# Batches 0 and 1 of a packed attention with routed experts: keys turned in thirds, values in one transfer a group

## The chip, the cores and the metric

The kernel runs on one core of one Trainium2 chip. The metric is the device time of one execution in microseconds, median of three runs. Of the engines, the TensorE (PE) multiplies and transposes, VectorE (DVE), ScalarE (ACT) and GpSimd (POOL) do the element work, and SyncE (SP) mostly issues DMA transfers.

## What is computed

Eight batches of attention with eight heads, 576 tokens of 64 columns, and 32 packed rows a head; then a mixture of experts over the 4608 rows, whose router picks one of 8 experts:

```python
def _attn_ref(q, k, v, p):                       # q, k, v: 8 x 8 x 576 x 64, p: 8 x 8 x 32 x 64
    p_packed = sm_attn(p, k, v)                  # packed rows attend to the tokens
    return sm_attn(q, p_packed, p_packed)        # tokens attend to the packed rows

def _moe_ref(x, expert_emb, tau, w1, w2):        # x: 4608 x 512, w1: 8 x 512 x 1024, w2: 8 x 1024 x 512
    xn, en = x / (norm(x) + 1e-6), expert_emb / (norm(expert_emb) + 1e-6)
    logits = xn @ en.T / tau
    expert_idx = argmax(logits)
    for e in range(8):
        h = maximum(x[mask(e)] @ w1[e], 0.0)
        out[mask(e)] = gate_w[mask(e), None] * (h @ w2[e])
```

## The kernel before

The kernel takes the batches one after the other. For each it guesses the one expert of the batch, loads that expert's weights and computes attention and the expert's two layers; a branch at the end repairs rows for which the guess was wrong. The expert's layers fill the TensorE (`ffn`: lines 1065, 1100, 1118), and the attention of the next batch is put between their matmuls, step by step, by tables (`PLAN` for batch 0) and counters. The order of every engine's instructions is the order in which the code records them.

Batches 0 and 1 start differently from the rest, in `begin`. Four heads form a group, and a batch has two groups. `load_whole` brings one group's keys (or queries) in one transfer of 576 KB into a tile `nat` of 128 partitions: a partition holds one head's 18 successive tokens, 64 columns each. The TensorE turns blocks of 128 columns (two tokens) of it into a PSUM bank (`turn`, line 1265), and ScalarE or VectorE copies the bank into `kT` (in the tile `spare`). `parity_scores` (line 1297) then multiplies the turned packed rows (`wp`, made by `scaled` and `packed_turn`) with the keys of one head, odd and even tokens apart. For batch 0 the keys are turned in nine blocks a group, four at a time (`turn_keys` with `blocks`, which gives the blocks in the order 0, 3, 6, 1, 4, 7, 2, 5, 8), so that a head's columns in `kT` come in 32s and nine such runs are read in a row. Then come the maxima (line 452), the exponentials (458), turns of these (473), and the products with the values (486), from which the packed rows, the guess of the expert (638, 653) and the loads of its weights (952, 960) follow. Before all this the TensorE runs two matmuls on a tile of ones (`WARM`, line 1253).

`load_v` brings a group's values for the products at line 486: a tile of 96 partitions of which each third of 32 comes in its own transfer of 192 KB, three a group. For batch 0 one of the three is issued on ScalarE's queue, all others on SP's. The values of batch 1 and its queries (`load_nat`, four transfers of 140 KB a tile to 32 partitions each) are issued on SP after the weights of batch 0's expert. VectorE turns those queries (`flip`, line 298, tile `kt`), and the TensorE scores them at line 277.

After its first stretch `begin` goes on in steps that `PLAN` places: it turns batch 1's keys with five banks and copies, all copies on ScalarE, and scores them, while the first layer's rows of batch 0 are made (`rows_w1`, line 1033).

PSUM banks: `pf` has three, `pu` one of one bank, `pt` two of two banks each. A bank that comes around again waits for its copy. Transfers issued on SP and ACT carry one of eight completion semaphores in turn (DMAHW0 to DMAHW7 below), and a transfer that takes one again waits on its engine for the landing of the one that had it before.

## Time and profile before

| | us |
|---|---|
| median of 3 runs | 412.96 (412.46 to 413.61) |
| the profiled execution | 413.71 |
| its span | 412.0 |
| TensorE busy | 403.6 (98%) |
| VectorE busy | 310.5 (75%) |
| ScalarE busy | 203.6 (49%) |
| GpSimd busy | 161.7 (39%) |

The span runs from the first to the last instruction of the profiled execution; times in the rows below count from its start. The busy time of the TensorE is that of its matmuls, whose ends are modelled, so waits of a few tenths of a microsecond can lie inside it. The chain that ended last is 89% TensorE work; 7% of it are DMA transfers, all of these in the first 50 us.

### The profile page before, as it was taken

Reading aid. Unit: us, or ns where it says so; the run is one execution under the profiler, and the core shown is the slowest. Engines: PE = TensorE matmul, PEld = TensorE weight load, DVE = VectorE, ACT = ScalarE, POOL = GpSimd, SP = SyncE. Lnnn points to the kernel's source line nnn. Section 1 sums busy time; section 2 is a strip of 40 time slices with the busy share of each in tenths; the row PEclk is TensorE's granted clock in tenths of the full one; section 3 lists DMA queues with packets and bytes.
Section 4 is the critical chain, followed back from the end, with each engine's and each line's share of the span. In section 5 each row is a group of like instructions: output and inputs, shape, how many; then the busy total and the mean of one; then the engine's idle time right before and its main releaser. Section 6 shows DMA issues by size and latency. Waiting matters only on the chain.

```text
span 412.0 us, 11101 instructions
## 1 busy us (share of the span) xinstructions
PE 403.6 (98%) x4012; PEld 322.5 (78%) x4013; DVE 310.5 (75%) x984; ACT 203.6 (49%) x507; POOL 161.7 (39%) x202
## 2 busy tenths in 40 slices
PE   8999999999999999999999999999999999999995
PEld 4758588797878978698786978789687987879785
DVE  3577888589996889779896899868897798836700
ACT  4677454763257622765138622667237641475201
POOL 2355802337503474047703375035730477030500
PEclk9999999999999999999999999999999999999999
DMA  8999888876699679985799768995798722910022
GB/s 226 334 331 214 218 279 297 218 203 183 227 333 241 170 192 336 286 205 139 222 396 234 181 167 273 324 234 136 210 335 281 203 60 81 391 35 19 9 61 56
DMA packets 42607, 87.93 MB, mean 213 GB/s; under 512 B 11690, under 2 KB 20906, under 8 KB 42546
## 3 DMA queue, kind: packets, MB, share of 16 engines
q1 hardware_dynamic: 35280, 61.44, 53.8%
q0 software_dynamic: 6720, 25.17, 16.7%
q10 hardware_dynamic: 546, 0.54, 0.6%
q8 instruction: 34, 0.56, 0.6%
q14 instruction: 27, 0.22, 0.2%
HBM read 77.68 MB, written 9.44 MB: 211 GB/s over the span
## 4 chain that ended last, share of the span: by engine, by line
PE 89%; DMA 7%; SPq 1%; issue 0%; DVE 0%; ACT 0%; DVEq 0%; ACTq 0%
PE pf L1118 43%; PE pf L1065 22%; PE pf L1100 6%; PE pt L995 3%; PE pt L797 3%; DMA w2r<-in_moe_w 2%; DMA vn<-in_v 2%; PE pt L403 2%; DMA nat<-in_q 2%; PE pt L277 2%; PE pt L338 2%; PE pu L797 2%; PE pf L1253 1%; PE pf L1265 1%; SPq L952 0%
## 5 line engine op out<-in xcount | busy, mean ns | idle before, releaser
L1118 PE MATMUL pf<-w2s,hT 128*128 128x512 f32 (+1 forms) x792 | 181.8, 387 | 0.0
L1118 PEld LDWEIGHTS pf<-w2s,hT 128*128 128x128 f32 x792 | 143.6, 188 | 39.2 <-issue 10.7
L971 POOL TENSOR_TENSOR w2s<-w2r,w2s 128x512 fp32r<-128x512 f32 x64 | 80.8, 1286 | 73.0 <-ACT w2s L970 68.2
L1065 PE MATMUL pf<-AT,G 128*128 128x288 f32 x720 | 102.1, 298 | 0.4 <-DVE hT L1070 0.2
L1065 PEld LDWEIGHTS pf<-AT,G 128*128 128x128 f32 x720 | 97.2, 188 | 4.3 <-issue 1.5
L1070 DVE SCALAR_TENSOR_TENSOR hT<-pf,hT 128x224 fp32r<-128x224 f32 (+1 forms) x128 | 52.2, 413 | 29.1 <-ACT hT L1069 28.7
L1069 ACT ACTIVATE hT<-pf 128x224 fp32r<-128x224 f32 (+1 forms) x128 | 49.2, 385 | 42.9 <-PE pf L1065 40.2
L298 DVE STREAM_TRANSPOSE kt<-nat 128x576 f32<-128x576 f32 x52 | 38.0, 757 | 2.3 <-DMA nat<-in_q 2.0
L1475 ACT ACTIVATE o<-pf,gate 128x512 f32<-128x512 f32 (+1 forms) x41 | 25.9, 633 | 24.6 <-PE pf L1118 17.1
L970 ACT CAST w2s<-w2r 128x512 fp32r<-128x512 f32 x64 | 37.7, 623 | 0.0
L891 POOL MEMSET oh<- 64x8 f32 x8 | 0.8, 98 | 86.1 <-DVE oh L887 86.1
L716 ACT ACTIVATE st<-st 128x576 f32<-128x576 f32 (+1 forms) x17 | 11.1, 658 | 43.7 <-DVE st L713 42.6
L1100 PE MATMUL pf<-w2r,h 128*64 128x256 f32 x256 | 31.5, 385 | 0.0
L1008 DVE TENSOR_TENSOR G<-pt,G 128x1024 fp32r<-128x1024 f32 x14 | 16.5, 1220 | 15.7 <-ACT G L1007 15.7
L933 ACT ACTIVATE lg<-lg 128x40 f32<-128x40 f32 x8 | 1.9, 237 | 48.4 <-DVE lg L929 48.4
L390 POOL TENSOR_TENSOR qs<-p 128x320 f32<-128x320 f32 x12 | 10.5, 876 | 36.9 <-ACT p L371 36.9
L1100 PEld LDWEIGHTS pf<-w2r,h 128*64 128x64 f32 x256 | 16.9, 137 | 8.5 <-PE pu L510 1.0
L810 ACT ACTIVATE scr<-pt 128x512 f32<-128x512 f32 (+1 forms) x32 | 15.7, 490 | 13.8 <-DVE part L851 10.6
L737 ACT CAST AT<-at 128x576 fp32r<-128x576 f32 x15 | 10.1, 674 | 17.9 <-DVE at L731 17.8
L371 ACT ACTIVATE p<-pt,qnm 128x160 f32<-128x160 f32 x48 | 17.7, 397 | 0.0
L960 POOL DMA_DIRECT2D w2r<-in_moe_w x24 | 17.0, 721 | 0.0
L702 DVE STREAM_TRANSPOSE st<-pt 128x288 f32<-128x288 f32 x32 | 13.3, 451 | 0.9 <-PE pt L1297 0.9
(235 smaller groups left out, 520.1 us busy)
## 6 DMA issues: line engine op xcount, KB each, us to landing
nat<-in_q SPq DMA_DIRECT2D x112, 140.0 KB, 3.4
nat<-in_k SPq DMA_DIRECT2D x96, 140.0 KB, 3.2
w1t<-in_moe_w POOLq DMA_DIRECT2D x12, 1024.0 KB, 7.1
w2r<-in_moe_w POOLq DMA_DIRECT2D x24, 512.0 KB, 9.6
out<-o SPq DMA_DIRECT2D x124, 64.0 KB, 2.3
w2r<-in_moe_w SPq DMA_DIRECT2D x8, 512.0 KB, 10.0
vn<-in_v SPq DMA_DIRECT2D x24, 160.0 KB, 3.8
vn<-in_v SPq DMA_DIRECT2D x48, 80.0 KB, 3.7
```

The source lines that it names most:

```text
L298: nc.vector.transpose(kt.rearrange("p (c i) -> p c i", i=32), t)
L371: nc.scalar.activation(x.p1[g][:, n * QW : n * QW + QW], area(x, g)[:, n // 2, n % 2], AF.Exp, bias=x.nm[:, at : at + 1],)
L797: nc.tensor.matmul(to, x.at[at, g, tokens], x.ppx[at, g], start=True, stop=True, tile_position=(64 * half, column),)
L960: queue.dma_start(t, w2e[:, 2 * i : 2 * i + 2, :])
L970: nc.scalar.copy(t[:, 0], raw)
L971: nc.gpsimd.tensor_tensor(out=t[:, 1], in0=raw, in1=t[:, 0].bitcast(F32), op=ALU.subtract)
L1065: nc.tensor.matmul(pf[:, :HS], w, r, start=(n == 0), stop=(n == len(ops) - 1))
L1069: nc.scalar.activation(hT[:, 0, f, cs], pf[:, :n], AF.Relu)
L1070: nc.vector.scalar_tensor_tensor(out=hT[:, 1, f, cs], in0=pf[:, :n], scalar=0.0, in1=hT[:, 0, f, cs].bitcast(F32), op0=ALU.max, op1=ALU.su ...
L1100: nc.tensor.matmul(pf[64 * hf : 64 * hf + 64, :256], h4[:, f], x.w2r[f // 2][:, f % 2, hf * 256 : hf * 256 + 256], start=(f == 0), stop=(f ...
L1118: nc.tensor.matmul(pf[:, :w], hT[:, a, f, c * P : (c + 1) * P], x.w2s[f][:, m, at : at + w], start=(f == 0 and i == 0), stop=(f == NF - 1 ...
L1475: nc.scalar.activation(o[:, :w], pf[:, :w], AF.Copy, scale=x.gate[:, c : c + 1])
```

## The change

Four things are changed, all in batches 0 and 1.

- `load_whole` can load a tile in two parts; batch 0's keys of group 0 come as columns 0 to 383 and the rest, those of group 1 as columns 0 to 767 and the rest.
- Keys are turned in thirds: three successive blocks of 128 go to one bank and one copy of 384 columns. Batch 0 then uses `one_bank` and `bank` in turn, batch 1 six banks instead of five. A head's columns are now read with a stride: `(a c r i)` as `c i a`, the third `a` innermost, 384 columns (1536 bytes) from one element to the next.
- `load_v` lays six successive tokens on a partition, and a group's 96 partitions come in one transfer of 576 KB on SP's queue.
- Order and size: the packed rows are turned first, the scores of group 0 stand ahead of the last third of group 1, and the second matmul of `WARM` has 128 columns instead of 512.

```diff
-    def load_whole(src, g):
+    def load_whole(src, g, split=0):
         t = sb.tile([P, NCB * D], F32, name="nat", tag="nat", bufs=4)
         s = src[g * HB : (g + 1) * HB].rearrange("h (i c) d -> h i (c d)", c=NCB)
-        nc.sync.dma_start(t, s.rearrange("h i w -> (h i) w"))
+        s = s.rearrange("h i w -> (h i) w")
+        for cs in (slice(0, split), slice(split, NCB * D)) if split else (slice(0, NCB * D),):
+            nc.sync.dma_start(t[:, cs], s[:, cs])
...
-    def load_v(b, g, odd=nc.sync):
+    def load_v(b, g):
         t = sb.tile([P, KC * HB * D], F32, name="vn", tag="vn", bufs=2)
         t = t.rearrange("p (h w) -> p h w", h=HB)
-        s = v[b, g * HB : (g + 1) * HB].rearrange("h (i c) d -> i h (c d)", c=NCB)
-        for a in (0, 2, 1):
-            (odd if a == 2 else nc.sync).dma_start(
-                t[32 * a : 32 * a + 32], s[:, :, a * KC * D : (a + 1) * KC * D]
-            )
+        s = v[b, g * HB : (g + 1) * HB].rearrange("h (p c) d -> p h (c d)", c=KC)
+        nc.sync.dma_start(t[:KR], s)
...
-        kn = [load_whole(k[0], g) for g in range(NG)]
+        kn = [load_whole(k[0], g, (g + 1) * 3 * P) for g in range(NG)]
...
-        vn = [load_v(0, g, nc.scalar) for g in range(NG)]
+        vn = [load_v(0, g) for g in range(NG)]
...
-        def parity_scores(to, w, t, g, at):
-            t = t[:, g].rearrange("p (c r i) -> p c r i", r=HB, i=32)
+        def parity_scores(to, w, t, at, g):
...
-                        t[hs, :, head(g, c)],
+                        t[hs, head(g, c)],
...
+        def turn_keys(nat, g, a, pu, copy):
+            turn(nat, pu, range(3 * a, 3 * a + 3))
+            copy(kT[:, g, 3 * a * P : 3 * a * P + 3 * P], pu[:, : 3 * P])
+
+        def key_scores(x, w, g):
+            t = kT[:, g].rearrange("p (a c r i) -> p r c i a", a=3, c=3, r=HB)
+            parity_scores(x.s1[g], w, t, lambda c: head(g, c), g)
+
+        wx = packed_turn(scaled(pn, nc.vector), one_bank())
...
-        for n in range(2 * NG):
-            if n:
+        for n in range(3 * NG):
+            turn_keys(kn1[n // 3], n // 3, n % 3, bank(), nc.scalar.copy)
+            if n not in (0, 3):
                 yield
-            pu = bank()
-            turn(kn1[n // 2], pu, blocks(n % 2 * 4, n % 2 * 4 + 4))
-            nc.scalar.copy(kT[:, n // 2, n % 2 * 512 : n % 2 * 512 + 512], pu)
...
-    WARM = (4, 4)
+    WARM = (4, 1)
```

The line numbers of the changed kernel are one to nine lower or higher than before from there on (1265 is 1264, 1297 is 1292, 1440 is 1307). Three places show what moves. The first is the TensorE's queue at the start, from the turn of the packed rows to the scores of batch 0's second group; `nat_130` and `nat_132` (`nat_133` after) are the keys of groups 0 and 1, `pt` the score banks. Before:

```order
L1283 MATMUL pu_193<-ident_75,wp_158 128x128 [waits DVE_49]
L1283 MATMUL pu_193<-ident_75,wp_158 128x128
L1265 MATMUL pf_197<-ident_75,nat_132 128x128 [waits DMAHW4_49,PE_49]
L1265 MATMUL pf_197<-ident_75,nat_132 128x128 x3
L1265 MATMUL pf_203<-ident_75,nat_132 128x128 [waits Activation_49]
L1265 MATMUL pf_203<-ident_75,nat_132 128x128
L1265 MATMUL pu_207<-ident_75,nat_132 128x128 [waits Activation_49]
L1265 MATMUL pu_207<-ident_75,nat_132 128x128 x2
L1297 MATMUL pt_177<-spare_157,wp_158 32x288 [waits DVE_49]
L1297 MATMUL pt_177<-spare_157,wp_158 32x288 x7
L1297 MATMUL pt_178<-spare_157,wp_158 32x288 [waits DVE_49,Activation_49]
```

And after:

```order
L1264 MATMUL pf_191<-ident_75,nat_130 128x128 [waits PE_49]
L1264 MATMUL pf_191<-ident_75,nat_130 128x128 x2
L1264 MATMUL pu_196<-ident_75,nat_133 128x128 [waits DMAHW5_49,Activation_49]
L1264 MATMUL pu_196<-ident_75,nat_133 128x128 x2
L1264 MATMUL pf_201<-ident_75,nat_133 128x128 [waits DVE_49]
L1264 MATMUL pf_201<-ident_75,nat_133 128x128 x2
L1292 MATMUL pt_179<-spare_155,wp_156 32x288 [waits DVE_49,Activation_49]
L1292 MATMUL pt_179<-spare_155,wp_156 32x288 x7
L1264 MATMUL pu_214<-ident_75,nat_133 128x128 [waits DMAHW6_49,Activation_49]
L1264 MATMUL pu_214<-ident_75,nat_133 128x128 x2
L1292 MATMUL pt_180<-spare_155,wp_156 32x288 [waits DVE_49,Activation_49]
```

The scores of group 0 have moved ahead of the last three turns of group 1, which wait for a part of their own (DMAHW6); the packed rows' turn has moved to the very start.

The second is SP's queue behind the last weight transfer of batch 0's expert: values (`vn`) and first queries (`nat`) of batch 1. Before:

```order
L960 DMA w2r_428<-in_moe_w2 128x2x512 [waits DMAHW7_49]
L232 DMA vn_430<-in_v 32x4x384 [waits DMAHW0_49,PE_49]
L232 DMA vn_430<-in_v 32x4x384 [waits DMAHW1_49]
L232 DMA vn_430<-in_v 32x4x384 [waits DMAHW2_49]
L232 DMA vn_434<-in_v 32x4x384 [waits DMAHW3_49,PE_49]
L232 DMA vn_434<-in_v 32x4x384 [waits DMAHW4_49]
L232 DMA vn_434<-in_v 32x4x384 [waits DMAHW5_49]
L201 DMA nat_438<-in_q 32x1120 [waits DMAHW6_49,PE_49]
L201 DMA nat_438<-in_q 32x1120 [waits DMAHW7_49]
```

And after:

```order
L959 DMA w2r_427<-in_moe_w2 128x2x512 [waits DMAHW5_49]
L233 DMA vn_429<-in_v 96x4x384 [waits DMAHW6_49,PE_49]
L233 DMA vn_431<-in_v 96x4x384 [waits DMAHW7_49,PE_49]
L201 DMA nat_433<-in_q 32x1120 [waits DMAHW0_49,PE_49]
L201 DMA nat_433<-in_q 32x1120 [waits DMAHW1_49]
```

Six transfers of values are two, so the first query transfer comes four transfers sooner; its semaphore was DMAHW6, that of the third second-layer weight transfer, and is now DMAHW0, that of the third first-layer one.

The third is ScalarE's queue where it copies batch 1's turned keys into `spare`, between the turned packed rows (`wp`) and the first layer's rows (`g`). Before:

```order
L1285 COPY wp<-pf 128x2x128 [waits PE_49]
L1434 COPY spare<-pf 128x2x128 [waits PE_49,Activation_49]
L1440 COPY spare<-pf 128x512 [waits PE_49]
L716 ACTIVATE st<-st 128x288 [waits Pool_49] x2
L1440 COPY spare<-pf 128x512 [waits PE_49] x3
L1045 COPY g_550<-pf 128x512 [waits PE_49] x2
```

And after:

```order
L1281 COPY wp<-pf 128x2x128 [waits PE_49]
L1307 COPY spare<-pf 128x384 [waits PE_49]
L1307 COPY spare<-pf 128x384 [waits PE_49,Activation_49]
L715 ACTIVATE st<-st 128x288 [waits Pool_49] x2
L1307 COPY spare<-pf 128x384 [waits PE_49]
L1307 COPY spare<-pf 128x384 [waits PE_49,Activation_49]
L1307 COPY spare<-pf 128x384 [waits PE_49]
L1307 COPY spare<-pf 128x384 [waits PE_49,Activation_49]
L1044 COPY g_547<-pf 128x512 [waits PE_49] x2
```

Five copies have become six of one size; two stand ahead of the softmax's exponentials as before, and four instead of three behind them.

## Rows read from the trace of the kernel before

**Rows 1.** Busy time by stage: us, busy (instructions) by engine, PEclk, DMA share, GB/s

```profile
36.00:48.00 12.00, 11.44 (x181) 9.45 (x180) 8.68 (x30) 8.10 (x20) 7.31 (x8) 1.00 0.89 240
...
100.00:148.00 48.00, 48.00 (x496) 38.84 (x494) 40.58 (x126) 23.87 (x60) 20.65 (x26) 1.00 0.79 233
```

**Rows 2.** TensorE timeline, first 52 us: start, length, instruction [idle before, releaser]

```profile
1.23 3.78 PE L1253 MATMUL pf<-fill 128*128 128x512 f32 x4 [1.23 <-DVE mask L72]
5.08 1.62 PE L1265 MATMUL pf<-ident,nat 128*128 128x128 f32 x8
...
7.99 1.36 PE L1297 MATMUL pt<-spare,wp 64*32 64x288 f32 x32
...
10.49 0.53 PE L473 MATMUL pt<-ident,p 128*96 128x128 f32 x3 [0.83 <-ACT p L458]
...
22.23 0.63 PE L1033 MATMUL pf<-w1t,tw 64*32 64x512 f32 x4 [0.53 <-ACT spare L1440]
...
34.04 3.82 PE L1065 MATMUL pf<-AT,G 128*128 128x288 f32 x24 [0.25 <-DVE hT L1070]
...
45.41 0.59 PE L510 MATMUL pu<-ident,ppx 128*128 128x128 f32 x2 [0.43 <-DVE ppx L500]
...
48.34 1.87 PE L277 MATMUL pt<-kt,T 64*32 64x288 f32 x32
```

**Rows 3.** TensorE timeline, the same group of matmuls for batch 2

```profile
100.66 1.20 PE L277 MATMUL pt<-kt,T 64*32 64x288 f32 x32
```

**Rows 4.** VectorE timeline: batch 0's maxima, two of batch 1's four query transposes

```profile
8.82 1.42 DVE L452 TENSOR_REDUCE mx<-pt 128x1 f32<-128x576 f32 x2 [0.62 <-PE pt L1297]
...
41.69 0.78 DVE L298 STREAM_TRANSPOSE kt<-nat 128x576 f32<-128x576 f32 x1 [1.24 <-DMA nat<-in_q]
...
48.22 0.78 DVE L298 STREAM_TRANSPOSE kt<-nat 128x576 f32<-128x576 f32 x1 [0.80 <-DMA nat<-in_q]
```

**Rows 5.** Chain of waits, 19 to 44 us: start, length, what

```profile
19.65 10.19 DMA w2r<-in_moe_w
...
29.85 10.03 DMA vn<-in_v
...
39.90 3.89 DMA nat<-in_q
```

**Rows 6.** Stages again, for the last two columns: DMA share, GB/s

```profile
12.00:17.00 5.00, 4.94 (x131) 4.43 (x131) 2.54 (x12) 2.85 (x8) 0.90 (x2) 1.00 1.02 393
...
31.00:34.00 3.00, 2.79 (x12) 1.84 (x10) 2.01 (x4) 2.76 (x8) 2.27 (x2) 1.00 1.10 195
36.00:44.00 8.00, 7.87 (x146) 7.37 (x146) 5.78 (x23) 6.50 (x18) 3.31 (x5) 1.00 0.88 234
```

**Rows 7.** SP's waits, first 60 us: total us, times, longest

```profile
SPq L201 <- DMA w2r<-in_moe_w: 4.7, 2, 2.4
```

**Rows 8.** SP timeline: first-layer weight and query transfers issued

```profile
16.63 2.14 SPq L952 DMA_DIRECT2D w1t<-in_moe_w  x4
...
32.65 11.47 SPq L201 DMA_DIRECT2D nat<-in_q  x16
```

**Rows 9.** DMA issues, whole span: size of one, median us to landing

```profile
w1t<-in_moe_w SPq DMA_DIRECT2D x4, 512.0 KB, 4.5
```

**Rows 10.** Line 1265 between 4 and 7 us: duration ns min/median/max, first and last start

```profile
L1265 PE MATMUL pf<-ident,nat x9: 273/414/444, 5.1 to 6.9; 128*128 128x128 f32 x9
```

**Rows 11.** Line 208, the keys' and queries' whole tiles

```profile
DMA to landing us min/median/max: 3.9/8.2/9.9
```

**Rows 12.** Line 1297, whole span: duration ns min/median/max, first and last start

```profile
L1297 PE MATMUL pt<-spare,wp x64: 402/403/427, 8.0 to 24.1; 64*32 64x288 f32 x64
```

**Rows 13.** ScalarE timeline: last key copy and second exponential of batch 0, batch 1's copies

```profile
8.10 0.48 ACT L1319 COPY spare<-pu 128x384 f32<-128x384 f32 x1
...
10.34 0.73 ACT L458 ACTIVATE p<-pt,mx 128x576 f32<-128x576 f32 x1
...
21.61 1.54 ACT L1440 COPY spare<-pf 128x512 f32<-128x512 f32 x3
```

38 lines of the change are left out of this document (13 added, 25 removed).

## The prediction

> **What bounds the kernel now.** I read the busy time by stage first. From 100 to 148 us the TensorE is busy 48.00 of 48.00 us, from 36 to 48 us only 11.44 of 12 [rows 1]. The change touches batches 0 and 1 alone, whose attention ends near 50 us, so what it can gain is what the TensorE loses before then, and a gain there should reach the end, because the later stages leave the TensorE no gap in which it could be given back. Second, the TensorE's timeline [rows 2]: the idle times in brackets are 0.83 us at 10.49 (for the first exponential), 0.53 at 22.23 (a copy of batch 1's keys on ScalarE), 0.25 at 34.04 and 0.43 at 45.41 (both for VectorE); and the 32 query-score matmuls of batch 1 at 48.34 take 1.87 us where the same group at 100.66 takes 1.20 [rows 3], so 0.67 us is hidden waiting. Third, why VectorE was late there [rows 4]: its transposes of batch 1's queries waited 1.24 us at 41.69 and 0.80 us at 48.22 for the queries to land. Fourth, the chain of waits says why these landed late [rows 5]: a weight transfer (10.19 us), then a values transfer (10.03 us from its issue), then queries, each issued only when an earlier one had landed.
>
> **Values of batch 1: three transfers of 32 partitions become one of 96.** The six transfers carry 6 x 192 KB = 1.18 MB. While they move (31 to 34 us) the DMA engines are full, share 1.10, at 195 GB/s; tiles over 128 partitions move at 393 GB/s with share 1.02 (12 to 17 us) [rows 6]. So 32-partition transfers cost twice as much per byte: 1.18 MB / 195 = 6.0 us; at 393 it would be 3.0. No row shows 96 partitions; these two are the bounds, and I take 300 GB/s, nearer to the wide one as 96 is nearer to 128: 3.9 us, so 2.1 us less. Batch 0's values get the same, which is worth nothing: they were there when asked for at 12.0 us.
>
> Fewer transfers also shift the completion semaphores. Before, the first query transfer of batch 1 took that of the third second-layer weight transfer, and SP waited for it: 4.7 us in two waits [rows 7], issue at 32.65 [rows 8]. Now it takes that of the second first-layer transfer, which is issued soon after 16.63 and lands 4.5 us (median) later [rows 8, 9], some 10 us sooner. So the query transfers stand right behind the values. From 36 to 44 us the DMA share is only 0.88 [rows 6]: 8 x 0.12 = 1.0 us of gaps can close even if the values move no faster. The queries come 1.0 us (slow bound) to 4.0 us (fast bound) earlier, 3.1 at my value; the two VectorE waits need 1.24 and 0.80, so both go. What is late next: at 45.41 the TensorE's own eight matmuls before the transpose, so only the 0.43 us of idle is won; at 48.34 the 0.67 us. **Term: -1.1 us** (bounds -0.7 and -1.1: at the slow bound the first wait is not quite gone). Batch 2's keys and batch 1's weights, queued on SP behind the queries, move forward too; no row shows the TensorE waiting for them.
>
> **Batch 0's keys in parts, turned in thirds.** Before, the first transpose waits for the whole first key tile: issue 1.01, landing 3.9 us later (the shortest in [rows 11]), start at 5.08. Eighteen key transposes and two of the packed rows follow to 7.99, then the scores to 9.35; the maxima run 8.82 to 10.24, the second exponential starts at 10.34 [rows 2, 4, 13]. After, the packed turn and the first third come before 4.9 us; the other two thirds wait for the same bytes as before. The early transposes are slow (414 ns median against 273 at best [rows 10]; eight take 1.62 us), so six from 5.0 cost 1.3 us, six more of group 1 about 0.7: near 7.1. Scores of group 0 take 1.36 / 2 = 0.68 and end near 7.9, 0.9 sooner. But then the last third of group 1 is turned (0.3), copied on ScalarE (0.48 for 384 columns [rows 13]) and only then scored (0.7): with about 0.2 for handing over, 9.6, no better than 9.35. So the first exponential gains 0.9 us, but the second, behind its maximum (0.75), starts between 10.1 and 10.4 instead of 10.34, and the transposes that wait for it gain 0.3 at best. The 0.83 us of idle is moved, not removed. I take 0.2 us at the point where the expert is guessed.
>
> **Batch 1's keys in thirds.** 2304 columns are copied either way, in five copies before, in six after. Three of 512 take 1.54 us [rows 13], 0.51 each or 1.0 ns a column: 2.3 us in all; six of 384 at that pace 2.3 us, at 0.48 each 2.9. The TensorE's 0.53 us at 22.23 is a wait for these copies, i.e. for a free bank; they start 0.2 us earlier, but a sixth bank is now taken ahead of the first-layer matmuls, so a later copy must be over. By that reckoning the start at 22.23 hardly moves and the 0.2 us is lost here. Batch 0's softmax does not pass through this spot, starts 0.2 us earlier, and at 34.04 the TensorE waits 0.25 us for VectorE behind that softmax's last step: there I count it again. **Term: -0.2 us** (bounds +0.6, if the copies take the longer time, and -0.8, the whole 0.83).
>
> **The strided read.** The key scores now read a moving operand with 1536 bytes between neighbours in the innermost run of three, where it was runs of 32 in a row. The trace has no such read; the nearest row is the scores that read those runs (403 ns median [rows 12]). **Taken at 0**: the runs of 32 with gaps between them already cost what the gapless reads of the query scores cost (32 records in 1.36 and 1.20 us with the same 288 columns [rows 2, 3]). A gain is excluded, since as many columns are streamed; the upper bound is rival (a).
>
> **Warm-up.** (4, 1) instead of (4, 4) cuts 3.78 us [rows 2] to 3.78 x 640 / 1024 = 2.4, ending near 3.6 instead of 5.01. It covered a wait for keys, so its removal is free; the cost, if any, is the clock (b).
>
> **Sum.** -1.1 - 0.2 = -1.3 us. The profiled execution took 413.71 us (span 412.0), 0.75 above the median of 412.96; -1.3 gives 412.4 there and 411.7 as median. A measurement of this kernel can tell about 0.3%, 1.24 us, from no change, so the forecast lies on that edge.
>
> **Rivals.** (a) *Slower: the stride costs.* If the strided run is read f times slower, each group of scores (0.68 us, two per batch) grows by 0.68 (f - 1). One of the four has slack, three are on the path: 2.04 (f - 1). At f = 1.6 the gain is gone, from f = 2.3 the kernel is slower by 0.3%; f = 2 gives 413.7, f = 3 gives 415.8, and if each of four neighbours that now come together must be fetched apart, f = 4, 417.8. For it: four column groups of the array read the same partitions at once. Against it: the 1.36 us above, with gaps at every 32nd element.
> The Trainium skill, "SBUF — State Buffer", section "Door 1: The DMA port swizzle" (its note on cachelines), says that accesses run at full rate only within a 16-byte line, four f32 wide, and that each step to a new line pays. By that rule f lies above 1 and this change ends slower or unchanged; no run here shows it yet.
> (b) *The clock rises later.* The early transposes ran at the lower of TensorE's two levels (414 ns against 273) after unbroken TensorE work from 1.23 us on. Now there is a gap of some 0.4 us before 5.0, and others after. If the clock stays low through the scores, nine transposes at 0.1 us and two groups of scores at 0.6 us more make 2.1 us, about half of it on the path: 412.7.
> (c) *The queries land no earlier*: a 96-partition transfer moves no faster and the gaps stay, which leaves -0.2: 412.8. Against it: the share of 0.88 and the issue that no longer waits.
> (d) *The early gain survives*: banks are free in time at 22.23, and 0.8 instead of 0.2 us reaches the end: 411.1.
>
> **How the numbers follow.** Forecast 0.56 (411.1 to 412.3), (a) 0.15, of it 0.04 at f = 4, (b) 0.12, (c) 0.09, (d) 0.08. The predicted time is 411.7. Leaving out f above 1.9 (0.08), the luckier end of (d) and the worst of (b) gives 410.9 to 413.4. Faster by over 0.3%: 0.65 of the forecast's share, and (d): 0.44. Slower by over 0.3%: f above 2.3 and what of (b) is worse than priced: 0.11. Within 0.3%: the rest, 0.45.
>
> **What would show it.** Right: VectorE's query transposes without a DMA wait, the group at 48.34 in 1.2 us, values of batch 1 landing within some 12 us of their issue at the most, the second exponential near 10.2. Wrong: score matmuls well over 427 ns (stride); transposes of 414 ns after 6.5 us (clock); first-layer matmuls well before 22 us (d). What I may have wrong most easily is the turn of the banks near 22 us, which the order of instructions shows but whose cost I could only work out.

## The result: slower by 1%

The changed kernel takes **416.9 us** (median of 5 runs, 416.78 to 418.24) against 412.96: a ratio of 1.0098, 95% interval 1.0081 to 1.0115, so 3.3 to 4.7 us more. The forecast was 411.7 with a range of 410.9 to 413.4; the sign was wrong as well as the size.

The profiled execution of the changed kernel took 418.24 us (span 416.3). That of the kernel before took 413.71 (span 412.0), longer than any of its five timed runs then (412.46 to 413.61); that matters further down. The line numbers of the changed kernel differ a little from those of the kernel before.

First TensorE's waits in the first 50 us (waited by, for whom: us in total, times, longest), which answer to the brackets of [rows 2]:

```profile
PE pu L1264 <- DMA nat<-in_k: 2.0, 1, 2.0
...
PE pf L1264 <- ACT spare L1307: 1.1, 1, 1.1
PE pt L472 <- ACT p L457: 0.7, 1, 0.7
PE pt L1292 <- ACT spare L1307: 0.6, 1, 0.6
PE pf L1264 <- DMA nat<-in_k: 0.4, 1, 0.4
```

New are 2.4 us of waiting for keys, and waits for ScalarE's copies of keys. TensorE's timeline of the same stretch shows the order (start, length, instruction, idle before it):

```profile
5.20 0.88 PE L1264 MATMUL pf<-ident,nat 128*128 128x128 f32 x6 [0.41 <-DMA nat<-in_k]
8.13 0.72 PE L1264 MATMUL pu<-ident,nat 128*128 128x128 f32 x3 [2.04 <-DMA nat<-in_k]
8.63 0.85 PE L1264 MATMUL pf<-ident,nat 128*128 128x128 f32 x3
9.41 1.21 PE L1292 MATMUL pt<-spare,wp 64*32 64x288 f32 x16
10.55 0.90 PE L1264 MATMUL pu<-ident,nat 128*128 128x128 f32 x3
12.03 0.89 PE L1292 MATMUL pt<-spare,wp 64*32 64x288 f32 x16 [0.57 <-ACT spare L1307]
```

Group 1's transposes wait until 8.13 for its keys, the second group's scores start at 12.03, and both groups were done by 9.35 before [rows 2]. In the same stretch the clock falls: the windows (us, then busy time and, in brackets, instructions of TensorE, granted clock, DMA share, GB/s) show it after two microseconds in which TensorE did almost nothing. The trace's own clock records have the lower level from 8.31 to 11.73 us.

```profile
6.00:8.00 2.00, 0.08 (x1) 1.00 0.93 245
8.00:10.00 2.00, 1.87 (x22) 0.58 1.10 217
10.00:12.00 2.00, 1.46 (x19) 0.57 1.12 217
```

The query scores of batch 1 are the place where the forecast saw its gain. They do take 1.20 us now, where [rows 2] had 1.87, and VectorE no longer waits for queries. But they stand at 51.30, not at 48.34:

```profile
51.30 1.20 PE L276 MATMUL pt<-kt,T 64*32 64x288 f32 x32
```

The lateness is 3.2 us when VectorE takes the largest logit for the guess of the expert (18.72 against 15.50), 3.6 us at the first-layer matmuls (25.82 against 22.23), and 3.0 us at these query scores. Behind them the whole program is 2.3 to 2.5 us late, to TensorE's last matmul (410.03 against 407.54). So some 1.3 us came back in this pair of executions, about what the forecast had hoped for; why that proves nothing is told below. The chain's last steps give the rest (start, length, what): the last write of the output tile, before and after.

```profile
407.63 0.46 ACT o L1475
```

```profile
410.13 0.46 ACT o L1466
```

It ends 3.9 us ahead of the end of the span before (412.0) and 5.7 us ahead of it after (416.3): the end of the program has become **1.8 us longer**, though nothing is computed there. Raw records of ScalarE at that place (start in us, instruction) show where:

```
before  409.66 COMPARE_BRANCH     410.12 EVENT_SEMAPHORE
after   412.11 COMPARE_BRANCH     415.02 EVENT_SEMAPHORE
```

The program ends with a branch over a part that is skipped with this data (line 1588, `tc.If(n_rest > 0)`). ScalarE takes 0.46 us from that branch to the next instruction before, 2.91 us after, and SP, which ends the program, waits for it. The page counts one transfer of instructions more on queue 14 (28 against 27). That holds over all the runs that follow: 28 in each kernel in which this branch is long (2.6 to 3.0 us), 27 in each in which it is short.

### The profile page after: what moved, and what is told of

Read it like the earlier page. It is cut to its first block, busy times and chain, and to the rows that moved or that the text cites. A ratio compares the mean times of both kernels' runs of the same rounds, so it can differ in the third digit from the quotient of the medians.

```text
span 416.3 us, 11097 instructions
## 1 busy us (share of the span) xinstructions
PE 403.8 (97%) x4012; PEld 322.8 (78%) x4013; DVE 309.8 (74%) x984; ACT 203.7 (49%) x508; POOL 161.7 (39%) x202
## 3 DMA queue, kind: packets, MB, share of 16 engines
q0 software_dynamic: 6720, 25.17, 16.6%
## 4 chain that ended last, share of the span: by engine, by line
PE 93%; DMA 2%; ACT 1%; DVE 1%; issue 0%; SPq 0%; POOL 0%; DVEq 0%; ACTq 0%
PE pf L1117 43%; PE pf L1064 25%; PE pf L1099 7%; PE pt L994 3%; PE pt L796 3%; PE pt L402 2%; PE pt L276 2%; PE pt L337 2%; PE pu L796 2%; DMA nat<-in_k 1%; PE pt L1292 1%; PE pf L1264 1%; PE pt L472 0%; PE pu L509 0%; PE pu L1264 0%
## 5 line engine op out<-in xcount | busy, mean ns | idle before, releaser
L1466 ACT ACTIVATE o<-pf,gate 128x512 f32<-128x512 f32 (+1 forms) x41 | 25.9, 634 | 24.9 <-PE pf L1117 17.3
L736 ACT CAST AT<-at 128x576 fp32r<-128x576 f32 x15 | 10.1, 675 | 17.8 <-DVE at L730 17.8
```

The lines of the kernel that those rows point to most:

```text
L1466: nc.scalar.activation(o[:, :w], pf[:, :w], AF.Copy, scale=x.gate[:, c : c + 1])
```

## The experiments

Each is compared with the kernel before on the same chip in the same hour (medians 412.9 to 413.3 there). "TensorE's end" is the end of its last matmul in the profiled execution (407.54 before, 410.03 after).

### The end of the program

**e8**: the kernel before, with a longer skipped part.

```diff
+                for c in range(NC5 - 1):
+                    nc.scalar.copy(acc[0][:, c], acc[1][:, c])
```

> The kernel before, with four more copies on ScalarE in the part that is skipped at the end; nothing that runs is changed. If the place of the instruction behind the jump sets the end, ScalarE now takes about 2.6 us for the jump as in the changed kernel, and the time rises by 1.5 to 2 us, to 414.5 to 415. If not, it stays at 413 within 0.7 us.

Measured: 414.96 us, ratio 1.0037 (1.0021 to 1.0054). ScalarE's branch takes 2.81 us (408.97 to 411.77), and the program ends 6.1 us behind TensorE's last matmul, in place of 4.5. Four copies that never run (seven more instructions of ScalarE in the built program) cost 0.9 to 2.2 us.

**e9**: the changed kernel, with ScalarE told of the branch ahead, as SP is.

```diff
-                tc.mark_branch_hint_location("rest", engines=[mybir.EngineType.SP])
+                tc.mark_branch_hint_location("rest", engines=[mybir.EngineType.SP, mybir.EngineType.Activation])
```

> The changed kernel, in which the mark that tells SyncE of the coming jump, some 10 us ahead of it, is given to ScalarE too (one instruction more on ScalarE). If the 2.6 us of ScalarE's jump are the fetch of code that isn't there yet, it is fetched ahead, the gap is near 0.5 us, and the time is 414.9 to 415.4. If the wait is something else, the time is that of the changed kernel within 0.7 us.

Measured: 415.42 us, ratio 1.0048 (1.0022 to 1.0074). The branch takes 0.48 us again (410.55 to 411.03) and the end 4.9 us. The built program puts the hint at its very start: it runs at 0.90 us, not some 10 us ahead of the branch as the expectation has it. That ScalarE has one instruction more by it is not the reason: e4 below has as many (611 in the main part) and a branch of 3.04 us. So the wait is for code that hadn't been brought in, and it makes about 1.5 us of the 4 (416.90 against 415.42 in the medians, 6.3 against 4.9 us at the end of the profiled executions). VectorE's branch over the same part takes 2.9 to 3.2 us in every kernel here, the one before included, but it begins 16 us ahead of TensorE's last matmul and is long over by the end. The Trainium skill, "Runtime: NRT & Kernel Launch", section "Instruction fetch mechanics", says that a taken branch to a target outside the two pages which the engine holds has to fetch the target's page before it goes on; the trace agrees in kind, with 2.9 us and one transfer of instructions more against 0.46; that the target lay outside two pages is not shown.

**e7**: the changed kernel, with a shorter skipped part (eight of its copies written for VectorE).

```diff
-        nc.scalar.copy(t[:, 0], raw)
+        (nc.vector.tensor_copy if SKIPPED else nc.scalar.copy)(t[:, 0], raw)
```

> The changed kernel; in the part of the program that is skipped at its end (for rows that no expert took, of which there are none here), eight copies are written for VectorE instead of ScalarE, so that ScalarE's jump over that part is eight instructions shorter. Nothing that runs is changed. If the 2.6 us that ScalarE takes from its branch to the instruction it lands on, against 0.46 in the kernel before, come from where that instruction lies (the changed kernel has one instruction of ScalarE more), the gap is back near 0.5 us, the program ends 4.5 us behind TensorE's last matmul in place of 6.3, and the time is 1.5 to 2 us below 416.9, at 414.9 to 415.4. If the gap has another cause, it stays at 2.5 us or more and the time is that of the changed kernel within 0.7 us.

Measured: 419.46 us (417.17 to 420.92), ratio 1.0138 (1.0082 to 1.0194). The branch still takes 2.79 us. So the simple theory falls that the landing place had moved one instruction too far. Over all runs the built programs show this: the branch was short (0.46 us) where ScalarE had at most 609 instructions in the main part and the skipped part was no longer than before, or with the hint; it was long in all others. Which boundary lies there stays open. Since nothing that runs was changed, e7 is also a second measurement of the changed kernel, and it shows that its early part isn't steady: 5.7 us above the kernel before, with an interval of 3.4 to 8.0. In its profiled execution 15 of batch 0's 18 key transposes, those up to 8.7 us, take over 400 ns (five in the kernel before), and TensorE's end is 410.83.

### Batch 0

**e12**: the kernel before with batch 0's part of the change alone.

```diff
-        kn = [load_whole(k[0], g) for g in range(NG)]
+        kn = [load_whole(k[0], g, (g + 1) * 3 * P) for g in range(NG)]
-        vn = [load_v(0, g, nc.scalar) for g in range(NG)]
+        vn = [load_v_one(0, g) for g in range(NG)]
...
+        third(kn[1], 1, 1, bank(), copies[1])
+        third_scores(x.s1[0], wx, 0)
+        pu = one_bank()
+        third(kn[1], 1, 2, pu, copies[0])
+        third_scores(x.s1[1], wx, 1)
-    WARM = (4, 4)
+    WARM = (4, 1)
```

> The kernel before with only batch 0's part of the change: keys in four transfers, the thirds and their order of copies and scores, the stride, the values in one transfer of 96 partitions a group, the short warm-up. If the loss is made in the first 20 us, TensorE is 2.5 to 3.5 us later than in the kernel before from there on and has no gain at 45 to 52 us: the last matmul at 409.7 to 411, the time 415.2 to 416.5 with a short jump at the end and 416.9 to 418.2 with a long one. If batch 0's part is neutral, the last matmul stays within 0.6 us of 407.54.

Measured: 415.12 us, ratio 1.0055 (1.0033 to 1.0076), TensorE's end 409.11, a short branch (0.46 us). The guess of the expert comes 3.1 us behind that of the kernel before, as in the changed kernel, and here too the clock is at its lower level, from 8.15 to 14.98 us. Batch 0's part is a loss of 1.4 to 3.1 us by itself. The next runs take it apart.

**e16**: of batch 0's part only the thirds, their order and the stride; whole keys, values in transfers of 32 partitions, long warm-up (the edit is shown against e12).

```diff
-        kn = [load_whole(k[0], g, (g + 1) * 3 * P) for g in range(NG)]
+        kn = [load_whole(k[0], g) for g in range(NG)]
-        nc.sync.dma_start(t[:KR], s)
+        for a in (0, 2, 1):
+            (odd if a == 2 else nc.sync).dma_start(
+                t[32 * a : 32 * a + 32], s[32 * a : 32 * a + 32]
+            )
-    WARM = (4, 1)
+    WARM = (4, 4)
```

> The kernel before with, in batch 0 alone, the turning in thirds, its order of copies and scores and the stride; keys in whole transfers, values in three transfers of 32 partitions a group, the long warm-up, and batch 1 as before. If the thirds make the early loss (the last third of group 1 is copied by ScalarE only behind the first group's scores), the second exponential stands 1 us or more behind that of the kernel before at 10.34, and the time is 413.6 to 414.6. If the loss comes from the keys' parts, the values' transfers and the warm-up, the second exponential is within 0.5 us of 10.34 and the time within 0.5 us of 413.

Measured: 414.88 us, ratio 1.0053 (1.0040 to 1.0066). Keys land as in the kernel before (5.13 and 7.04 us), the clock is at its upper level from 6.29 us on (6.23 in the kernel before), and still the second exponential starts at 11.67 in place of 10.34 [rows 13]. TensorE's and ScalarE's timelines show the order at work:

```profile
7.95 0.88 PE L1325 MATMUL pt<-spare,wp 64*32 64x288 f32 x16
8.77 0.55 PE L1275 MATMUL pu<-ident,nat 128*128 128x128 f32 x3
9.88 0.89 PE L1325 MATMUL pt<-spare,wp 64*32 64x288 f32 x16 [0.57 <-ACT spare L1318]
```

```profile
9.35 0.48 ACT L1318 COPY spare<-pu 128x384 f32<-128x384 f32 x1 [1.14 <-PE pu L1275]
...
11.67 0.74 ACT L468 ACTIVATE p<-pt,mx 128x576 f32<-128x576 f32 x1 [1.10 <-DVE mx L462]
```

The last third of group 1 is turned at 8.77, behind the first group's scores, copied at 9.35, and only then can the second group be scored; its maximum and exponential come behind that. The loss is as large as that of e12, all of batch 0's part (1.0053 and 1.0055).

**e18**: e16 with that third ahead of the scores, and group 1's first third in another bank; nothing else.

```diff
-        third(kn[1], 1, 0, one_bank(), copies[0])
+        third(kn[1], 1, 0, bank(), copies[0])
         third(kn[1], 1, 1, bank(), copies[1])
-        third_scores(x.s1[0], wx, 0)
         pu = one_bank()
         third(kn[1], 1, 2, pu, copies[0])
+        third_scores(x.s1[0], wx, 0)
```

> The run with thirds and stride alone in batch 0, but all three thirds of group 1 are turned and copied ahead of the first group's scores, as the kernel before turns its blocks. If that order made the 2 us, the second exponential comes at 10.4 to 10.9 in place of 11.67 and the time is 413.0 to 413.8. If the stride made it, the second exponential stays at 11.3 or later and the time at 414.5 or more.

Measured: 413.49 us, ratio 1.0016 (1.0003 to 1.0029). The scores run in one go, and the second exponential comes 0.73 us behind the first (it was 1.93 in e16), though here the keys landed 0.35 us later than there and moved both.

```profile
8.62 1.54 PE L1325 MATMUL pt<-spare,wp 64*32 64x288 f32 x32
```

```profile
10.41 0.74 ACT L468 ACTIVATE p<-pt,mx 128x576 f32<-128x576 f32 x1 [1.20 <-DVE mx L462]
...
11.14 0.73 ACT L468 ACTIVATE p<-pt,mx 128x576 f32<-128x576 f32 x1
```

So **the order of that one third costs about 1.5 us** (1.0053 against 1.0016, each with an interval of 0.0013 on either side); what stays of batch 0's part, above all the stride and the natural order of the keys, costs 0.1 to 1.2.

**e1**: the changed kernel, with the copies writing each key where the scores want it.

```diff
-            copy(kT[:, g, 3 * a * P : 3 * a * P + 3 * P], pu[:, : 3 * P])
+            to = kT[:, g].rearrange("p (r c i a) -> p a c r i", r=HB, c=3, i=32)[:, a]
+            copy(to, pu[:, : 3 * P].rearrange("p (c r i) -> p c r i", c=3, r=HB))
```

> The changed kernel, but the copies that empty the turned keys put each key where the scores want it, 12 bytes apart, so that the score matmuls of batches 0 and 1 read 288 neighbouring columns again. Nothing else differs. If the stride is what made the kernel slower (rival a with a factor of 2 or more), the time falls from 416.9 by 2 us or more. By the trace of the changed kernel the strided matmuls take 486 to 507 ns at the full clock, where the contiguous ones of the kernel before took 402: then 16 matmuls that run four at a time save about 0.3 us in each batch, and 416.3 to 416.9 is expected, with score matmuls back at 402; a copy that writes with a stride may give that back by taking longer than it did.

Measured: 418.95 us (416.79 to 419.9), ratio 1.0147 (1.0112 to 1.0182): no gain. The score matmuls' own rows (duration ns min/median/max, first and last start, forms), after and in e1:

```profile
L1292 PE MATMUL pt<-spare,wp x64: 486/497/686, 9.4 to 27.9; 64*32 64x288 f32 x64
```

```profile
L1292 PE MATMUL pt<-spare,wp x64: 402/403/687, 8.2 to 26.7; 64*32 64x288 f32 x64
```

The stride makes a matmul 497 ns in place of 403, a factor of 1.23, and without it they are back at 403. But ScalarE's copy of 384 columns, 0.48 us in [rows 13], takes 0.66 to 0.68 in e1 with its strided write: the cost is only moved. The one run of e1 at a mean granted clock of 0.996 took 416.79 us, as the changed kernel does; the other three, at 0.983 to 0.990, took 418.18 to 419.90.

**e17**: the kernel before with batch 0's keys in four transfers, and nothing else.

```diff
+        for cs in (slice(0, split), slice(split, NCB * D)) if split else (slice(0, NCB * D),):
+            nc.sync.dma_start(t[:, cs], s[:, cs])
...
-        kn = [load_whole(k[0], g) for g in range(NG)]
+        kn = [load_whole(k[0], g, (g + 1) * 3 * P) for g in range(NG)]
```

> The kernel before with batch 0's keys in the changed kernel's four transfers, and nothing else. If the parts make group 1 late, its second part lands at 7.5 to 9 us in place of 6.75 for the whole, the first exponential comes 1 us or more behind 9.61, and the time is 413.6 to 414.6. If the parts alone cost nothing, the time is within 0.5 us of 413.

Measured: **419.87 us** (415.34 to 420.17), ratio 1.0154 (1.0124 to 1.0184). The two parts of group 1 land at 8.72 and 9.54 us, where the whole landed at 6.75, and TensorE waits:

```profile
PE pf L1267 <- DMA nat<-in_k: 3.0, 3, 2.5
```

The profiled execution (415.34) was the best of six, with a mean granted clock of 0.996. The four at 419.8 to 420.2 had 0.985 to 0.988: there the wait was followed by a fall of the clock, it seems, and that costs more than the wait. They have no trace of their own. In the profiled execution no fall is recorded, though TensorE stood idle for 2.52 us.

**e3** and **e4**: the changed kernel with whole keys, and the changed kernel with batch 0's values in three transfers of 32 partitions a group, one of them from ScalarE.

```diff
-        kn = [load_whole(k[0], g, (g + 1) * 3 * P) for g in range(NG)]
+        kn = [load_whole(k[0], g) for g in range(NG)]
```

> The changed kernel with batch 0's keys in one transfer a group, as before. If the four transfers themselves hold the keys of group 1 up (their issues on SyncE, and the wait for the first part), group 1 lands near 6.75 us again in place of 7.99 and 8.99, and the time falls by 1 us or more, to 415.9 or less. If the values behind them in the queues hold them up, group 1 lands at 8 to 9 us here too, and the time stays within 0.5 us of 416.9.

```diff
-        nc.sync.dma_start(t[:KR], s)
+        for a in (0, 2, 1) if odd else ():
+            (odd if a == 2 else nc.sync).dma_start(t[32 * a : 32 * a + 32], s[32 * a : 32 * a + 32])
```

> The changed kernel, with batch 0's values brought in as before by three transfers of 32 partitions a group, the second of them issued by ScalarE; batch 1's stay in one transfer a group. If the one transfer over 96 partitions takes the DMA engines from the keys of group 1, these land near 6.75 us again, TensorE's wait for them of 2 us goes with most of the fall of the clock, and 414 to 415.5 is expected. If the split of the keys or the stride is to blame, group 1 still lands at 8 us or later and the time stays within 0.5 us of 416.9.

Measured: e3 417.54 us (ratio 1.0099, 1.0065 to 1.0132), e4 420.47 us (1.0182, 1.0151 to 1.0213). In e3 group 1 lands at 7.36, but TensorE waits 1.1 us for each group's keys (group 0's land whole at 5.19, in place of 3.6 and 5.2 in parts) and the clock falls as well (0.50 from 8 to 10 us). In e4 its parts land at 8.85 and 10.92, and the clock is at its lower level from 8 to 18 us. So the values' single transfer is not what holds the keys up: with the keys in parts it is the **three** transfers that do, as in e17. One transfer a group repairs a good part of that damage, and no more. In the five kernels with the changed kernel's transfers the second part of group 1 landed between 7.45 and 8.99 us from one execution to the next.

**e2** and **e13**: the warm-up, long in the changed kernel, short in the kernel before.

```diff
-    WARM = (4, 1)
+    WARM = (4, 4)
```

> The changed kernel with the longer run of empty matmuls of the kernel before (4 and 4 blocks in place of 4 and 1). If the clock that fell at 8.31 us and came back at 11.73 is a part of the loss, it stays up, the 3.4 us of work in that stretch take about half of it, and 415.2 to 416.2 is expected, with the granted clock at full from some 5 or 6 us on. If only the late keys of group 1 matter, TensorE waits for them either way and the time is within 0.5 us of 416.9.

> The kernel before with the short warm-up alone (4 and 1 blocks in place of 4 and 4). If the short warm-up by itself lets TensorE's clock fall, half level shows somewhere between 4 and 12 us and the last matmul comes 1 us or more later. If the fall in the changed kernel needed the wait for group 1's keys as well, the clock stays at full and the time is within 0.6 us of 413.

Measured: e2 416.29 us (ratio 1.0077, 1.0048 to 1.0105), clock 1.00 in every window from 6 to 12 us; e13 414.07 us, ratio 1.0032 (1.0017 to 1.0046), although in its profiled execution (413.56, the best of five) TensorE's end is 407.48. The short warm-up alone thus costs 0.7 to 1.9 us. The trace has 1.6 us of idle TensorE ahead of the first transposes, where the long warm-up ran, and then a first run of eight that takes 1.94 us in place of 1.62 [rows 2]:

```profile
5.34 1.94 PE L1265 MATMUL pf<-ident,nat 128*128 128x128 f32 x8 [1.60 <-DMA nat<-in_k]
```

The windows print a clock of 1.00 here, but also where the trace has no clock record yet, and its first record, at the upper level, begins at 8.35 us (6.23 in the kernel before). The lengths of the transposes between 4 and 9 us (ns min/median/max) tell the level ahead of it: 421 ns, which is also what they take in the changed kernel where its clock is recorded at the lower level. First the kernel before, then e13:

```profile
L1265 PE MATMUL pf<-ident,nat x14: 272/287/444, 5.1 to 7.5; 128*128 128x128 f32 x14
```

```profile
L1265 PE MATMUL pf<-ident,nat x14: 272/421/448, 5.3 to 8.6; 128*128 128x128 f32 x14
```

So the clock rises later here. The scores start 1.62 us behind the landing of group 1's keys (9.10 and 7.48), where the kernel before has 1.24 (7.99 and 6.75): some 0.4 us. What makes the rest of the 0.7 to 1.9 is not shown. In the kernels with the long warm-up the first record begins at 4.2 to 7.2 us; with the short one it begins at 4.3 to 5.3 us in five, and at 8.35 (e13), 9.23 (e1) and 9.80 (e7) in three.

**c1**: the changed kernel with the edits of e1, e2, e3 and e4 together.

> The changed kernel with four of its parts undone together: keys of batch 0 in whole transfers, its values in three transfers of 32 partitions a group (one on ScalarE), the long warm-up, and scores that read neighbouring columns. What stays changed is the turning in thirds and batch 1's values in one transfer. If the early loss comes from these four (late keys of group 1, the clock, the stride), group 1's keys land near 6.75 us, the clock holds, and TensorE ends 1 to 2 us earlier than in the kernel before (its last matmul at 405.5 to 406.7 us against 407.54): with the longer end of the program, 6.3 us after that matmul in place of 4.5, that is 412.5 to 414.5. If the thirds themselves cost the time, TensorE ends no earlier than in the kernel before and the time is 414.5 or more.

Measured: 416.97 us, ratio 1.0084 (1.0054 to 1.0113), TensorE's end 408.19, no fall of the clock recorded. That is the time of the second theory: undoing the four together gives back nothing that the median shows, though the edit of e1 among them makes copies longer. What is left of batch 0's part, the thirds, is taken apart above, in e16 and e18.

### Batch 1

**e10**, **e11** (and **e14**, the same kernel again): the kernel before with batch 1's part alone, with six copies, and with the five copies of before in natural order (the edit shown is that of e11; e10 has the changed kernel's loop of six copies in place of its second cut).

```diff
-            loaded[1, 2 * NPR + g] = load_v(1, g)
+            loaded[1, 2 * NPR + g] = load_v_one(1, g)
...
-            turn(kn1[n // 2], pu, blocks(n % 2 * 4, n % 2 * 4 + 4))
+            turn(kn1[n // 2], pu, range(n % 2 * 4, n % 2 * 4 + 4))
...
-            parity_scores(y.s1[g], wy, kT, g, lambda c: head(g, c))
+            third_scores(y.s1[g], wy, g)
```

> The kernel before with only batch 1's part of the change: its keys turned in thirds by six copies and read with a stride, its values in one transfer a group. If the loss sits in batch 0's part and in the end of the program, batch 1's part brings the waits of VectorE on the queries down (1.65 us came back between 45 and 52 us in the changed kernel) and costs 0.7 to 1.1 us for the sixth copy on ScalarE, which TensorE waits for: its last matmul comes 0.5 to 1.0 us earlier than in the kernel before, at 406.5 to 407.0. The time is then 412.0 to 412.8 if the jump at the end is short as before, 413.7 to 414.6 if it is long. If batch 1's part is itself a loss, the last matmul comes at 407.5 or later.

> As the run on batch 1's part alone, but with the five copies of the kernel before (blocks 0 to 3 and 4 to 7 of each group, and the two last blocks together), now in natural order. If the sixth copy costs TensorE 0.7 to 1.1 us, the last matmul comes that much earlier than with six copies, at 405.9 to 406.2; if the number of copies doesn't matter, it comes within 0.3 us of the one with six. The time is 411.3 to 412.0 with a short jump at the end and 413.0 to 413.7 with a long one.

Measured: e10 415.59 us (ratio 1.0063, 1.0045 to 1.0081) with a long branch (2.95 us), e11 414.14 (1.0029, 1.0014 to 1.0044) with a short one (0.46), e14 413.66 (1.0033, 1.0020 to 1.0046; 413.5 to 414.5 was expected). TensorE's end is 408.26 in e10, 407.46 in e11 and 406.32 in e14. The expectations, 406.5 to 407.0 and 405.9 to 406.2, were missed, and e11 and e14, which are one kernel, lie further apart than e10 and e11: the ends of single executions can't price the sixth copy, nor can the medians, which differ by about the branch. A shorter stretch can. From the guess of the expert to the first-layer matmuls it is 7.1 us in all seven kernels with six plain copies (18.72 to 25.82 in the changed one) and 6.7 to 6.8 us in ten with five (15.50 to 22.23 before); e16, with 7.5, is the exception. So **six copies in place of five cost 0.3 us** there. In the changed kernel the wait for a bank has moved to the last transposes of batch 1's keys and is 1.09 us, in place of 0.53 ahead of the first-layer matmuls [rows 2]:

```profile
25.34 0.55 PE L1264 MATMUL pf<-ident,nat 128*128 128x128 f32 x3 [1.09 <-ACT spare L1307]
25.82 0.63 PE L1032 MATMUL pf<-w1t,tw 64*32 64x512 f32 x4
```

And batch 1's part, the only source of the forecast's gain, is itself **slower** than the kernel before.

**e15**: e14 with each group's values of batch 1 in three transfers again (the edit is shown against e14).

```diff
-        nc.sync.dma_start(t[:KR], s)
+        for a in (0, 2, 1):
+            nc.sync.dma_start(t[32 * a : 32 * a + 32], s[32 * a : 32 * a + 32])
```

> The partner: the same kernel, but each group's values of batch 1 come in three transfers of 32 partitions, as in the kernel before. If the one transfer brings the queries sooner (the forecast's 1.1 us), this kernel is about 1 us slower than its partner, 414.5 to 415.5, with VectorE waiting 1 to 2 us on the queries at 38 to 50 us. If the one transfer gives nothing (it takes as long as the three together) the two are within 0.4 us of each other. If it holds the queries up, this one is faster by 0.5 us or more, 412.6 to 413.6.

Measured: 413.14 us, ratio 1.0006 (0.9995 to 1.0016), beside 413.66 and 1.0033 for the partner. Three transfers are the better ones, by 0.4 to 1.8 us as the two ratios go; the natural order and the stride of batch 1 cost nothing that can be measured (at most 0.7 us). The rows of the values' transfers between 20 and 45 us say why one brings nothing (last line of each: from issue to landing, of one transfer); first the kernel before, then e15, then e14:

```profile
L232 SPq DMA_DIRECT2D vn<-in_v x6: 311/312/1112, 21.8 to 29.9; - x6
DMA to landing us min/median/max: 10.0/12.4/14.4
```

```profile
L242 SPq DMA_DIRECT2D vn<-in_v x6: 311/312/479, 21.9 to 29.2; - x6
DMA to landing us min/median/max: 9.4/11.2/12.8
```

```profile
L241 SPq DMA_DIRECT2D vn<-in_v x2: 452/1434/2417, 21.2 to 22.0; - x2
DMA to landing us min/median/max: 14.4/15.5/16.5
```

From the first issue to the last landing that is 18.1 us before (21.78 to 39.89), 16.6 in e15 (21.94 to 38.58) and 17.3 in e14 (21.22 to 38.56). Over all the kernels it is 16.3 to 18.1 us with three transfers and 15.2 to 19.8 with one. In the changed kernel the DMA engines are full all the while (36 to 44 us: share 1.01 in place of 0.88) and move the same bytes a second, 233 GB/s against 234 [rows 6]:

```profile
36.00:44.00 8.00, 7.79 (x52) 6.87 (x51) 6.76 (x21) 5.76 (x17) 5.02 (x5) 1.00 1.01 233
```

A single execution's rate says little, though: e8, with the transfers of the kernel before, moves 274 GB/s in that window. Why the one transfer makes a slower kernel than three is not settled. 0.3 us of it lies at the end of the program in the profiled executions (4.78 us behind TensorE's last matmul in e11 and e14, 4.46 in e15), with a short branch in all three. In e11's trace VectorE waits 1.2 us for queries, in e14's it doesn't wait at all.

### What is left of the change

**e19**: the changed kernel with whole keys, the long warm-up, all thirds of group 1 ahead of the scores, five copies for batch 1, and values of both batches in transfers of 32 partitions.

> The changed kernel with what the runs point to: keys in whole transfers, values of both batches in three transfers of 32 partitions, the long warm-up, all thirds of group 1 ahead of the scores, and five copies for batch 1. Of the change there remain the natural order of the keys, the stride, and contiguous rows of the values. ScalarE then has as many instructions ahead of the last jump as the kernel before, so the jump should take 0.46 us. If the losses are the ones named, the time is 412.8 to 413.8, no better than the kernel before; below 412.5 something of the change pays; at 414.5 or more a loss is not yet found.

Measured: 413.67 us, ratio 1.0014 (0.9999 to 1.0029), with a short branch (0.46 us; ScalarE has 609 instructions in the main part again). No loss can be told from zero any more (at most 1.2 us), and no gain appears. No version here beats the kernel before.

## Why the prediction was wrong

Both terms of the sum failed, the -1.1 and the -0.2, and two costs stood at nothing: the strided read and the end of the program.

**The -1.1 us for batch 1's queries.** This step failed twice. First, the rate: 300 GB/s was taken for 96 partitions, between the 195 and 393 of [rows 6]. A tile of 96 partitions came no faster (15.2 to 19.8 us from first issue to last landing, where three transfers took 16.3 to 18.1). The rival (c) named this and got 0.09; its price, 412.8, still counted no loss. Closing the gaps in the DMA share, the second argument, happened (0.88 to 1.01) and moved no more bytes. The queries' issue did come earlier, at 27.81 in place of 32.65, as worked out from the semaphore (the text calls it that of the second first-layer transfer; it is the third's), and the first of them landed later, at 41.74 in place of 40.37.

Second, and worse, **the wait that was to go comes and goes from one execution to the next, with three transfers and with one**. VectorE's 1.24 and 0.80 us of [rows 4] come from one execution, a longer one than the five that were timed with it. In other kernels whose batch 1 values still come in three transfers VectorE's idle time ahead of the same two transposes is 0.00 and 0.00 (e8 and e16), 0.00 and 0.15 (e15), 0.43 and 0.38 (e13), but 0.42 and 1.54 in e19. In kernels with one transfer it is 0.00 and 0.00 (e2 and e14), but 0.31 and 0.90 (e11), 0.51 and 1.34 (e10), and 1.59 and 0.45 (e7). The last of the four transposes in e8 and in e19 (the bracket's name of a transfer is inferred; what the transpose waits for is its last query transfer):

```profile
47.40 0.78 DVE L298 STREAM_TRANSPOSE kt<-nat 128x576 f32<-128x576 f32 x1
```

```profile
48.74 0.78 DVE L298 STREAM_TRANSPOSE kt<-nat 128x576 f32<-128x576 f32 x1 [1.54 <-DMA pn<-in_p]
```

Of e8, which runs exactly what the kernel before runs up to its end, TensorE's end was 406.94, 0.6 us ahead of 407.54. The prediction noted that its profiled execution was 0.75 us above the median, and still took the whole term off the median; most of that wait may never have been in it. So "VectorE's query transposes without a DMA wait" and "the group at 48.34 in 1.2 us", which the text named as signs that the step is right, came true in the changed kernel and in e8 alike, and prove nothing. Its other two signs of being right failed: the values landed 12.2 and 14.6 us behind their issue, and the second exponential started at 13.81 us.

**The -0.2 us for batch 0's keys.** The bounds were -0.8 and +0.6, and the early loss was 3.2 us at the point where the expert is guessed (18.72 against 15.50); batch 0's part alone cost 2.3 us (e12). Four pieces of the working failed, the second of them the dearest (about 1.5 us, e16 against e18):
- "The other two thirds wait for the same bytes as before": group 1's parts landed at 7.99 and 8.99, not at 6.75 (e17 alone: 8.72 and 9.54).
- "9.6, no better than 9.35" for the end of the second group's scores: e16, with the keys in time, ends them at 10.77. The row of steps was right (turned, copied, scored), but it was started at 7.9 from the end of the first scores, where e16 has 8.77; the second exponential is at 11.67, not at 10.1 to 10.4.
- "Its removal is free" for the warm-up: 1.3 us (e13), when it is the only change.
- "The start at 22.23 hardly moves": the sixth copy adds 0.3 us there, within the bound of +0.6. The text had named this turn of the banks as its weakest place.

What the keys' parts and the short warm-up cost when put in alone (7.0 us in e17, 1.3 in e13) is not what they cost in the changed kernel: e12, with both, and e16, with neither, lie within each other's intervals.

**The stride at 0.** The rival (a) had the right formula with f open: f is 497 / 403 = 1.23, so 2.04 x 0.23 = 0.5 us, and e18, which has it in batch 0 alone, measured 0.1 to 1.2. The evidence taken for zero (runs of 32 with gaps cost as much as none) did not carry over to runs of three elements 1536 bytes apart. The rule that the prediction takes from the Trainium skill, "SBUF — State Buffer", section "Door 1: The DMA port swizzle", that each step to a new line pays, did foresee a cost, and the trace agrees with that much; the prediction's extreme of f = 4 is far off. Its own sign for this, score matmuls well over 427 ns, came true.

**The clock, rival (b)**, was priced at 1.0 us with a chance of 0.12. Its mechanism is there, in some executions: the late rise that it names stands in the traces of e13, e1 and e7, and its reading of the slow early transposes as the lower level was right. Its sign, transposes of 414 ns after 6.5 us, came true as well (421 ns, up to 11.0 us). In the changed kernel's own profile the clock rose early (4.90 us) and fell later, after the wait for keys, which no term had. By the mean clocks that fall is not in the median: of the five runs the two with a mean granted clock of 0.993 and 0.994 took 417.91 and 418.24 us, the three with 0.996 to 0.998 took 416.78 to 416.90. If a fall is what sets e17's runs apart, it cost some 4 us there (415.3 and 415.9 against 419.8 to 420.2). For that speaks e4, whose trace has the lower level for 10.2 us at a mean of 0.986, as low as in e17's four; against it, one run of e4 took 420.33 at a mean of 0.998.

**The end of the program** was in no term and in no rival: 1.5 us by e8's ratio, 1.8 in the profile.

The parts don't add exactly: batch 0 alone 2.3 us (e12), batch 1 alone 1.2 (e11) and the branch 1.5 (e8) make 5.0 of the 4.0 measured, whose interval reaches to 4.7. The difference is no larger than the intervals of the three.

## What to carry to other kernels

Before a wait becomes a term of a forecast, ask whether it is there in every execution; a profile of one long run shows waits that others don't have, and a start that is late for another reason can make them vanish as well. Ask of every reordering which copy then stands between two pieces of the matrix engine's work: one third turned behind the scores in place of ahead of them cost about 1.5 us, more than the whole forecast gain of 1.3. And when a change moves even one instruction of an engine that ends with a branch, look at the end of the program before the middle is blamed; a branch hint for that engine is a single line.

## What the runs showed of the hardware

- Four copies more in code that never runs made the program 1.5 us slower (e8); a hint at the program's start took the 2.9 us of ScalarE's jump back to 0.48 (e9). Each kernel with the long jump has one transfer of instructions more than those with the short one (28 against 27).
- Splitting 1152 KB of keys into four transfers ahead of six values transfers made the last bytes land at 9.54 us in place of 6.75, and the program 7 us slower in the median, 2.5 us in its best run (e17).
- A float32 matmul with 288 columns took 497 ns where the innermost three elements lay 1536 bytes apart, and 403 ns without that stride (e1).
- After 2.0 us with TensorE idle its granted clock was 0.58 and 0.57 in the next two windows of 2 us, the lower of its two levels for most of them (1.2 in place of 2.4 GHz). Not every pause did that: the clock fell behind one of 1.1 us in e3 and within one of 3.1 us in e4, while behind one of 1.3 us in e9 and one of 2.5 us in e17 no fall is recorded.
- A key transpose of 128 columns took 421 ns at the lower level and 273 at the upper one (the changed kernel, before and after its recorded changes). In e13 the lower one lasted to 8.35 us, with a printed clock of 1.00, because nothing is recorded there.
